# Attention and a Fourier feed-forward block: 120 matmuls of a constant tile added to the plan of the first phase

## The chip, the cores and the metric

The kernel runs on one core of a Trainium2 chip. The metric is the device time of one execution in microseconds (us); the median of several executions counts. An execution with the hardware profiler on left the profile that is read here.

## The reference, cut to what matters

```python
# q, k, v: (8, 8, 576, 64); w_ch1: (512, 2048); w_ch2: (2048, 512); everything in float32
kv  = einsum('bhsd,bhse->bhde', k, v)
out = einsum('bhsd,bhde->bhse', q, kv)
x   = out / sqrt(mean(out * out, -1) + 1e-6) * g_norm      # then (8, 576, 512)
X   = fft(fft(x, axis=1), axis=2)                          # over rows, then over columns
u   = x + real(X)
un  = (u - mean(u)) / sqrt(var(u) + 1e-6)
return u + maximum(un @ w_ch1, 0) @ w_ch2
```

## The kernel before

There are eight batches of 576 rows. For each batch the first phase does these steps. `plan_kv` loads k and v in four pairs of heads (L460) and multiplies them into `ps_k` (L481); the buffers of these loads are a ring of six, `RINGS["kv"]`. `plan_q_load` and `plan_q` load q in two sides (L504, L510), turn it on TensorE into `ps_q` (L529), and copy it on ACT (L533). `plan_out` multiplies it with kv into `ps_o` (L554); ACT copies and squares that (L569, L574), DVE sums it (L578), POOL multiplies it by the norm weights (L589). `plan_y` works out the root, `plan_fold` scales the rows and folds them by their symmetry: DVE (L651, L662), POOL (L669), then ACT makes the rounded half `xh` (L675) and POOL the rest `xl` (L678). `plan_seq` is the DFT over rows (`ps_f`, L693), `plan_chn` that over columns (L727), and `plan_turn` turns the result (`ps_t`, L813) into the blocks `unTh` and `unTl` for the feed-forward part.

The weights arrive as raw 64-bit numbers and are decoded on ACT (L285) and DVE (L292 to L302, L857), centred by a mean on TensorE (`ps_w`, L315), and split in two parts. Each feed-forward product is three fp32r matmuls (`passes`): `ffn1` (L354) makes `ps_h`, `ffn2` (L372) makes `acc`. `plan_early` does the first three of sixteen weight blocks for a block of 512 rows inside the first phase, as work that fills holes: its rank is `FILL + 10 * j` with `FILL = 1000`, while the steps of a batch have ranks from 0 to 77. After the first phase a plain loop does the rest.

The order of the first phase is made by `Plan`. Each step has an engine, a cost in ns, a rank, the steps it comes after, and the ring buffers it takes. `Plan.run` goes forward in time: whenever an engine is free it gives it the ready step of the lowest rank whose buffers are free, and emits that step's instructions. A step on another engine becomes ready `HOP` = 150 ns after the last step that it waits for. So the order on each engine follows from these costs. Tile's scheduler then keeps this order but for single instructions that are ready earlier than those ahead of them. Each engine runs its queue in order, and SP issues nearly all loads and stores.

All PSUM tiles are one ring of eight banks (`p8`, by `bank_buf`).

Of the kernel before, what the change touches and what calls it, by code (L numbers as in the profile page):

```python
# [10 lines left out]
F32R = mybir.dt.float32r  # L11
# [16 lines left out]
NA = 3  # L28
NB1 = 4
NSEG = 4  # L30


SLACK = 2000
# [23 lines left out]
class Plan:  # L57
# [16 lines left out]
    def op(self, eng, cost, rank, emit, after=(), bufs=(), lag=0, port=False, wait=0):  # L74
        o = Op()
        o.port = port or eng == "POOL"
        o.wait = wait
        o.eng, o.cost, o.rank, o.emit, o.lag = eng, cost, rank, emit, lag
        o.after = [a for a in after if a is not None]
        o.bufs = list(dict.fromkeys(bufs))  # L80
        for b in o.bufs:
            b.left += 1
        o.n = len(self.ops)
        o.done, o.dma = None, False
        self.ops.append(o)
        return o

    def dma(self, kb, rank, emit, after=(), bufs=(), eng="SP"):
        o = self.op(eng, 600, rank, emit, after, bufs, lag=kb * 4)
        o.dma = True  # L90
        return o
# [94 lines left out]
def kernel(  # L186
# [14 lines left out]
    nc = tc.nc  # L201
# [3 lines left out]
    P = 128  # L205
# [8 lines left out]
    KC = DM // P  # L214
# [24 lines left out]
    op, dma = plan.op, plan.dma  # L239

    def bank(name):
        return psum.tile([P, BT], F32, name=name, tag="p8", bufs=8)

    def bank_buf(name):
        return Buf("p8", lambda: bank(name))

    ident = perm.tile([P, P], F32, name="ident")
# [137 lines left out]
    cst = ph1.enter_context(tc.tile_pool(name="cst", bufs=1))  # L385
    one = ph1.enter_context(tc.tile_pool(name="one", bufs=1))
    two = ph1.enter_context(tc.tile_pool(name="two", bufs=2))

    gb = cst.tile([P, D], F32, name="gb")
    cs = cst.tile([TR + 1, 2, 2, 3, NS], F32R, name="cs")  # L390
    cd = cst.tile([P, 2, 2, 2, ND], F32R, name="cd")
    x0 = cst.tile([TR + 1, 3, B], F32, name="x0")
# [8 lines left out]
    def rank(b, stage):  # L401
        return 10 * b + stage

    KV, QT, OUT, SCL, FOLD, SEQ, CHN, NRM = range(8)
    URGENT = -100
    FILL = 1000
# [5 lines left out]
    i_gb = dma(32, rank(0, QT), lambda: nc.sync.dma_start(gb, g_norm.partition_broadcast(P)))  # L412
    i_row = dma(18, rank(2, 0), lambda: nc.sync.dma_start(rowidx, order))

    dft = {}

    def plan_dft(part, dst, src, n, r, key):
# [680 lines left out]
    F1 = NA + NB1  # L1098
    early = [NBLK - 2, NBLK - 1] + list(range(NBLK - 3, NBLK - 1 - NSEG, -1))
    blocks = early[::-1][: len(early) - 2] + early[:2] + list(range(1, NBLK - NSEG)) + [0]  # L1100
    segs = [(j, NA, F1) for j in early]
# [197 lines left out]
```

## Time and profile before

| | us |
|---|---|
| median of 3 runs | 1025.22 |
| lowest, highest | 1022.89, 1028.03 |
| the profiled execution | 1026.22 |
| its span, from the first to the last instruction | 1024.4 |
| PE busy in it | 993.9 |
| DVE, ACT, POOL busy | 472.0, 322.4, 320.6 |

PE is TensorE's matmul, PEld its weight load, DVE is VectorE, ACT ScalarE, POOL GpSimd, SP SyncE; SPq and ACTq are the DMA issues of these engines. L481 is line 481 of the kernel. The views used are the page's totals; a table of stages, with the busy time of each engine in each stretch of the span; the timeline of an engine, which merges instructions that follow each other; and the chain of work that ended last, followed back from the end. Matmuls are pipelined, so the durations of single ones overlap; the distance from one start to the next is their pace. A matmul of 64 columns in float32 appears as two instructions.

### The profile page before, as it was taken

How to read it: one execution, taken by the hardware profiler on the slowest of the kernel's cores; microseconds unless marked ns; L12 is line 12 of the kernel's file. 1: busy time of each engine (PE TensorE's matmuls, PEld its weight loads, DVE VectorE, ACT ScalarE, POOL GpSimd, SP SyncE). 2: the span in 40 equal slices, each digit the busy share in tenths (PEclk: the TensorE clock that was granted, in tenths of full speed). 3: DMA queues.
4: the chain of work that ended last, by engine and by line, in shares of the span. 5: the costliest groups of instructions: out<-in, count | busy, mean ns of one | idle time of the engine just before them, and what ended most of it. 6: DMA issues, size and time to landing. Idle time of an engine off the chain costs nothing.

```text
span 1024.4 us, 15026 instructions
## 1 busy us (share of the span) xinstructions
PE 993.9 (97%) x5866; PEld 839.4 (82%) x5866; DVE 472.0 (46%) x838; ACT 322.4 (31%) x655; POOL 320.6 (31%) x332
## 2 busy tenths in 40 slices
PE   4698999999999999999999999999999999999998
PEld 4697898889888888888888888888888888888886
DVE  4758775654588689998131314131221311311211
ACT  2456565555545434334221212021121021210110
POOL 0555876864865131225722303020020010110000
PEclk9998999999999999999999999999999999999999
DMA  9979979663246766645552515140320400400101
GB/s 245 253 164 280 190 214 263 168 182 139 88 162 212 275 206 253 228 136 175 155 177 74 182 51 170 71 139 1 125 81 0 165 21 1 164 1 1 42 1 41
DMA packets 109194, 140.70 MB, mean 137 GB/s; under 512 B 51790, under 2 KB 76418, under 8 KB 104516
## 3 DMA queue, kind: packets, MB, share of 16 engines
q1 hardware_dynamic: 105588, 132.28, 42.4%
q0 software_dynamic: 1920, 6.29, 2.0%
q10 hardware_dynamic: 1616, 1.18, 0.4%
q8 instruction: 46, 0.75, 0.3%
q14 instruction: 24, 0.20, 0.1%
HBM read 88.33 MB, written 51.40 MB: 136 GB/s over the span
## 4 chain that ended last, share of the span: by engine, by line
PE 93%; DMA 2%; DVE 2%; SPq 1%; issue 1%; ACT 0%; POOL 0%; DVEq 0%; ACTq 0%; POOLq 0%
PE ps_h L354 38%; PE acc L372 38%; PE ps_o L554 4%; PE ps_f L727 3%; PE ps_f L693 3%; PE ps_k L481 3%; PE ps_q L529 2%; PE ps_t L813 2%; DMA vm<-in_v_dram 2%; DVE x L651 1%; DMA qt<-in_q_dram 1%; SPq L510 1%; PE ps_w L315 0%; SPq L460 0%; DVE unTl L825 0%
## 5 line engine op out<-in xcount | busy, mean ns | idle before, releaser
L354 PE MATMUL ps_h<-unTh,w 128*128 128x512 f32 x1152 | 357.1, 391 | 0.0
L372 PE MATMUL acc<-w,hh 128*128 128x512 f32 x1152 | 345.0, 391 | 0.2 <-DVE unTl L825 0.2
L367 DVE SCALAR_TENSOR_TENSOR hl<-ps_h,hh 128x512 fp32r<-128x512 f32 x144 | 99.2, 689 | 379.8 <-ACT hh L364 377.5
L354 PEld LDWEIGHTS ps_h<-unTh,w 128*128 128x128 f32 x1152 | 215.4, 188 | 44.0
L372 PEld LDWEIGHTS acc<-w,hh 128*128 128x128 f32 x1152 | 214.9, 188 | 44.3 <-issue 0.3
L364 ACT ACTIVATE hh<-ps_h 128x512 fp32r<-128x512 f32 x144 | 85.9, 597 | 472.1 <-PE ps_h L354 442.9
L354 PE MATMUL ps_h<-unTl,w 128*128 128x512 f32 x576 | 224.5, 390 | 0.0
L372 PE MATMUL acc<-w,hl 128*128 128x512 f32 x576 | 213.1, 390 | 0.0
L354 PEld LDWEIGHTS ps_h<-unTl,w 128*128 128x128 f32 x576 | 108.3, 188 | 22.7
L372 PEld LDWEIGHTS acc<-w,hl 128*128 128x128 f32 x576 | 107.9, 188 | 22.5
L1133 POOL DMA_INDIRECT uu<-u_scr,rowidx x24 | 23.4, 974 | 286.2 <-DVE uu L1186 175.6
L589 POOL TENSOR_TENSOR x<-x,gb 96x512 f32<-96x512 f32 (+1 forms) x48 | 61.9, 1308 | 55.2 <-ACT x L569 40.6
L1152 POOL TENSOR_TENSOR uu<-uu,up 128x512 f32<-128x512 f32 x36 | 45.7, 1293 | 44.5 <-ACT up L1149 44.5
L554 PEld LDWEIGHTS ps_o<-kvt,fq 64*96 64x96 f32 (+1 forms) x768 | 42.7, 185 | 5.6 <-issue 3.2
L554 PE MATMUL ps_o<-kvt,fq 64*96 64x64 f32 (+1 forms) x768 | 47.0, 274 | 0.3 <-ACT fq L533 0.3
L481 PE MATMUL ps_k<-vm,km 128*64 128x64 f32 x512 | 28.7, 261 | 17.6 <-DMA vm<-in_v_dram 16.7
L1096 POOL TENSOR_TENSOR w<-wap,w 128x512 fp32r<-128x512 f32 x18 | 23.3, 1295 | 70.1 <-ACT w L1095 70.1
L1186 DVE SCALAR_TENSOR_TENSOR uu<-acc,rs_yb,uu 128x512 f32<-128x512 f32 x36 | 25.2, 745 | 42.5 <-PE acc L372 42.5
L578 DVE TENSOR_REDUCE ss<-ps_o 96x8 f32<-96x512 f32 (+1 forms) x48 | 32.2, 682 | 26.2 <-ACT ps_o L574 26.0
L669 POOL TENSOR_TENSOR xe<-ab 96x256 f32<-96x256 f32 (+1 forms) x48 | 37.5, 803 | 19.8 <-DVE ab L662 19.7
L693 PE MATMUL ps_f<-cs,xh 96*128 96x290 f32 (+1 forms) x192 | 41.8, 312 | 0.4 <-DVE x L651 0.4
L481 PEld LDWEIGHTS ps_k<-vm,km 128*64 128x64 f32 x512 | 22.9, 166 | 22.4 <-DMA km<-in_k_dram 16.2
(103 smaller groups left out, 1009.1 us busy)
## 6 DMA issues: line engine op xcount, KB each, us to landing
raw<-in_moe_w_ch_dram SPq DMA_DIRECT2D x32, 512.0 KB, 7.6
qt<-in_q_dram SPq DMA_DIRECT2D x16, 576.0 KB, 9.2
unT_scr<-unTh SPq DMA_DIRECT2D x9, 1024.0 KB
unT_scr<-unTl SPq DMA_DIRECT2D x9, 1024.0 KB, 6.3
part_scr<-part SPq DMA_DIRECT2D x36, 256.0 KB, 4.1
unTh<-unT_scr SPq DMA_DIRECT2D x9, 1024.0 KB, 4.9
unTl<-unT_scr SPq DMA_DIRECT2D x9, 1024.0 KB, 7.0
up<-part_scr SPq DMA_DIRECT2D x36, 256.0 KB, 3.0
```

The lines of the kernel that those rows point to most:

```text
L354: nc.tensor.matmul(ps, w[c][:, kc * P : (kc + 1) * P], unT[a][:, kc, :], start=(idx == 0), stop=(idx == 3 * KC - 1),)
L364: nc.scalar.activation(hh, ps, AF.Relu)
L367: nc.vector.scalar_tensor_tensor(hl, ps, 0.0, hh.bitcast(F32), ALU.max, ALU.subtract)
L372: nc.tensor.matmul(acc, hpair[a][:, i * P : (i + 1) * P], w[c], start=(first and n == 0), stop=(last and n == 2),)
L481: nc.tensor.matmul(ps.t[s * D : (s + 1) * D, pr * D : (pr + 1) * D], km[:, s, j, :] if j < 4 else kr[:, h, :], vm[:, s, j, :] if j < 4 els ...
L554: nc.tensor.matmul(pss[s].t[:n, at : at + D], fqs[side].t[half, m, :n], kvt.t[half, m], start=True, stop=True,)
L578: nc.vector.tensor_reduce(ss.t[0][:n, :, t, s::2], pss[s].t[:n].rearrange("p (u m e) -> p u m e", u=2, e=D), AX.X, ALU.add,)
L589: nc.gpsimd.tensor_tensor(v_, v_, gb[:n].unsqueeze(1).to_broadcast([n, H, D]), ALU.mult)
L669: nc.gpsimd.tensor_tensor(o[:, s], a[:, 0], a[:, 1], ALU.subtract if s else ALU.add)
L693: nc.tensor.matmul(ps.t[:, :NS], xs[t].t[a][:n, part, ch * P : (ch + 1) * P], cs[:n, part, c, t, :], start=(idx == 0), stop=(idx == 8),)
L727: nc.tensor.matmul(ps.t[:n, :ND], pt.t[a][:, part, ch, offs[t] : offs[t] + n], cd[:, part, c, ch, :], start=(idx == 0), stop=(idx == 5),)
L1152: nc.gpsimd.tensor_tensor(us[j][i], us[j][i], part, ALU.add)
```

## The change

A step `TICK` of 12000 ns on an engine of its own and a copy of the identity into the tile `still` on DVE are what 60 new PE steps wait for. Each does two matmuls of `still` with itself, repeated four times along the columns. All write one bank: `ps` is made once, taken by the first of them and given back after the last. Their cost is 454 ns, their rank `FILL * 20` = 20000, above that of all others. Nothing reads that bank. The new steps come into being ahead of all steps of the batches.

```diff
+SPARE = 60
+SPARE_FROM = 12000
...
+    still = cst.tile([P, P], F32R, name="still")
...
+    def plan_spare():
+        i_still = op("DVE", 200, URGENT, lambda: nc.vector.tensor_copy(still, ident))
+        bell = op("TICK", SPARE_FROM, 0, lambda: None)
+        ps = bank_buf("ps_s")
+        wide = still.unsqueeze(1).to_broadcast([P, KC, P])
+
+        def go():
+            for _ in range(2):
+                nc.tensor.matmul(ps.t, still, wide, start=True, stop=True)
+
+        for _ in range(SPARE):
+            op("PE", 454, FILL * 20, go, [i_still, bell], [ps])
+
+    plan_spare()
```

## Rows read from the trace of the kernel before

**Rows 1.** The page: busy time of PE, and the granted clock by slice.

```profile
PE 993.9 (97%) x5866; PEld 839.4 (82%) x5866; DVE 472.0 (46%) x838; ACT 322.4 (31%) x655; POOL 320.6 (31%) x332
...
PEclk9998999999999999999999999999999999999999
```

**Rows 2.** Table of stages: stretch, length, busy us of engines, PEclk, DMA share, GB/s.

```profile
45.39:66.30 20.91, 20.91 (x173) 18.96 (x174) 10.39 (x17) 11.68 (x26) 13.27 (x14) 1.00 1.00 218
...
88.96:91.99 3.03, 0.00 (x1) 0.03 (x1) 3.00 (x6) 3.03 (x7) 1.32 (x2) 0.71 0.96 302
91.99:97.00 5.01, 5.01 (x36) 4.49 (x37) 5.01 (x10) 2.55 (x7) 1.80 (x2) 0.50 0.98 341
97.00:1024.40 927.40, 921.50 (x5065) 774.57 (x5064) 409.52 (x732) 273.71 (x550) 278.06 (x278) 1.00 0.40 128
```

**Rows 3.** PE's timeline: start, us, line, tiles, count, idle before and its releaser.

```profile
12.77 1.12 PE L481 MATMUL ps_k<-vm,km 128*64 128x64 f32 x16 [0.89 <-DMA km<-in_k_dram]
...
18.86 2.16 PE L529 MATMUL ps_q<-ident,qt 97*128 97x97 f32 x12 [4.55 <-DMA qt<-in_q_dram]
...
45.39 1.12 PE L481 MATMUL ps_k<-vm,km 128*64 128x64 f32 x16 [8.27 <-DMA vm<-in_v_dram]
...
91.99 1.12 PE L481 MATMUL ps_k<-vm,km 128*64 128x64 f32 x16 [3.03 <-DMA vm<-in_v_dram]
```

**Rows 4.** Chain that ended last, up to 110 us: start, us, what, instructions.

```profile
27.32 5.43 PE ps_o L554 x64
...
46.93 2.76 PE ps_q L529 x16
...
54.30 1.46 PE ps_k L481 x20
...
69.78 1.75 PE ps_k L481 x40
...
80.29 0.66 PE ps_q L529 x8
...
84.39 1.50 PE ps_o L554 x32
85.89 0.82 PE ps_t L813 x8
```

**Rows 5.** PE's timeline in the DFT over rows: its start, the rise, its end.

```profile
60.64 0.85 PE L693 MATMUL ps_f<-cs,xh 97*128 97x290 f32 x2
...
66.35 0.30 PE L693 MATMUL ps_f<-cs,xl 96*128 96x290 f32 x1
...
67.96 0.29 PE L693 MATMUL ps_f<-cs,xl 96*128 96x290 f32 x1
```

**Rows 6.** PE's timeline in feed-forward matmuls: the first ones, and ones from the middle.

```profile
95.34 1.20 PE L354 MATMUL ps_h<-unTh,w 128*128 128x512 f32 x2
96.34 0.63 PE L354 MATMUL ps_h<-unTl,w 128*128 128x512 f32 x1
...
800.92 0.62 PE L354 MATMUL ps_h<-unTh,w 128*128 128x512 f32 x2
...
811.12 0.62 PE L354 MATMUL ps_h<-unTh,w 128*128 128x512 f32 x2
```

**Rows 7.** Timelines of SP, DVE, ACT and POOL; the load is from the chain.

```profile
35.48 4.74 SPq L460 DMA_DIRECT2D km<-in_k_dram  x1
...
40.27 4.99 DMA vm<-in_v_dram
...
12.44 0.70 DVE L292 TENSOR_SCALAR ps_a<-ps_a 128x512 f32<-128x512 f32 x1 [11.38 <-ACT ps_a L285]
...
50.35 1.14 ACT L675 ACTIVATE xh<-xe 97x512 fp32r<-97x512 f32 x2
...
57.84 1.26 POOL L678 TENSOR_TENSOR xl<-xe,xh 96x512 fp32r<-96x512 f32 x1
```

## What I expect of the change

> **What bounds the kernel now.** I read the page's totals first, then a table of stages, then PE's timeline and the chain that ended last. The totals say that PE is busy nearly all the time [rows 1], so the end is set by PE's work plus what PE loses. The stage table says where it loses [rows 2]: from 97 us on PE is busy for 921.50 of 927.40 us, and most of the rest is the tail behind the last matmul. So all that matters lies ahead of 97 us, and a shift of the first feed-forward matmuls is a shift of the end.
>
> Ahead of 97 us there are two kinds of loss. The first is idle time: the four large waits are 0.89, 4.55, 8.27 and 3.03 us, all for loads [rows 3]. The second isn't seen in the busy time: pace. The chain gives it, start to end of a run of matmuls [rows 4]. A pair of kv (20 instructions) takes 1.46 us at 54 us and 1.75/2 = 0.875 at 70. A transpose takes 2.76/16 = 0.172 us at 47, and 0.66/8 to 0.82/8, some 0.09, after 80. An out instruction takes 5.43/64 = 0.085 us at 27 and 1.50/32 = 0.047 at 84. The sequence DFT shows the moment: 23 matmuls from 60.64 to 66.35 at 0.248 us each, then 12 in 1.61 us, 0.134 each [rows 5]. That is the 1.2 GHz level against the 2.4 GHz level. The page's clock row prints nearly full speed there [rows 1], and so does the stage table for 45.39 to 66.30 [rows 2]; I go by the pace, which doubles at 66.35 with no change of shape. So TensorE runs at half clock from its first matmul to 66.35 us, and again from some 91 to 97, after the idle 3.03 us, where the table does print 0.50 [rows 2].
>
> On that clock row the Trainium skill (TensorE: Matmul & The Clock Gate, Part 1, Seeing it yourself) warns that recorded clock events have been unreliable on trn2 and are to be checked against other figures; the pace above agrees. The same part (What's actually happening) holds the loss from warming up to be under 1% of a typical span. By that rule the half clock would be worth at most some 10 us here instead of the 17.0 below, and the sum would come out some 7 us slower (an estimate from that page).
>
> **The change part by part.** It adds 60 planner steps of two 128x128 by 128x512 matmuls, 120 in all; one copy of 128x128 on DVE, which sits idle until 12.44 us, so I cost it at nothing (without that cover, a quarter of the 0.70 us that a 128x512 step takes [rows 7]); 512 bytes a partition; and one PSUM bank that all 60 share, held from the first to the last. By the planner's own count at least three of the eight banks are free up to plan time 49, so the bank costs nothing (without that, an out step, which takes two, would be put off by the time of a copy and a square on ACT). Nothing reads the result, so no engine waits for it. What the spares cost is their place in PE's queue: q, out and kv of batches 0 and 1 stand behind them.
>
> *What one costs.* The feed-forward matmuls have this shape: 45 of them from 800.92 to 811.12, 0.2267 us each at full clock; at half clock two took 1.00 us, 0.50 each [rows 6]. 120 x 0.2267 = 27.2 us. The first run at half clock. How long until it rises is bounded by two rows: the DFT ran 5.7 us before it rose [rows 5], the feed-forward matmuls from 95.34 some 1.5 us [rows 6]. That is 3 to 11 matmuls with an excess of 0.27 us, 0.8 to 3.1 us. I take 2.0, since the spares have the shape of the second and come, as the first, after a long stretch at half clock. So 29.2 us.
>
> *Where they go.* Their rank is below all else and a step of 12000 holds them back, so the planner puts them into every hole of its PE from plan time 12.15 us on, 0.454 us each, rounded up. Its holes, worked out from its own costs, in order: ahead of the last kv pair of batch 0 (5 steps), between that and the first q (10), among q, out and the weight mean of batch 0 (3, 2, 6), ahead of the four kv pairs of batch 1 (8, 4, 8, 4), around q of batch 1 (6, 4). That is 60: they are used up at plan time 47, far ahead of the first feed-forward step at plan time 87. So none guards the wait of 3.03 us, and that loss stays. Since they wait for nothing once they have the bank, Tile's scheduler can only pull them ahead of these places; as the sum is made at q of batch 1, with nearly all of them past, that changes it little.
>
> *What they meet.* The first 15 steps take 30 x 0.2267 + 2.0 = 8.8 us and find 0.89 + 4.55 = 5.4 us of idle [rows 3]: q starts 3.4 us late, but at full clock. From there to the end of batch 1's third kv pair, at 37.06, PE had no idle worth the name, and gets 31 steps, 14.1 us. In return its work there runs at full clock: three kv pairs save 1.8 us, 24 transposes 2.0, 96 out instructions 3.6, a weight mean 0.4: 7.8 [rows 4]. Does the clock hold through such small matmuls? From 76.2 to 88.9 us PE does nothing but q, out, kv and transposes and one weight mean, at the fast pace to the end [rows 4], so yes. PE then reaches the fourth pair, with its 4 steps (1.8 us), at 37.06 + 3.4 + 14.1 - 7.8 + 1.8 = 48.6 instead of 45.39: the 8.27 us are filled and PE is 3.2 late. Ten more steps add 4.5. The work up to 66.35 saves 1.8 (kv), 2.0 (q), 64 x 0.038 = 2.4 (out), 0.4 and 23 x 0.114 = 2.6 (DFT): 9.2. By PE alone it is 3.2 + 4.5 - 9.2 = 1.5 us ahead at that point.
>
> *What is late next.* The DFT needs xl, which POOL finishes for the third row tile at 57.84 + 1.26 = 59.1, only 1.5 us before PE takes it up; POOL waits for xh on ACT, and on ACT xh (50.35) stands behind the copies of batch 1's transposes [rows 7]. Those start 3.2 + 2.7 = 5.9 us later (six of the ten steps stand ahead of them), so xl ends near 65.0. From there PE has 28 DFT matmuls left at 0.134, to 68.8, against 68.1 before (67.96 and one more). What PE had won turns into a wait for POOL of 2.2 us. **Sum: +29.2 (spares) - 17.0 (clock) - 13.7 (idle filled) + 2.2 (new wait) = +0.7 us.**
>
> *The loads.* The kv ring has six buffers, so the load of batch 1's fourth pair waits for its first pair on PE, which ended at 34.1 and now ends at 39.5 (3.4 late, 19 steps or 8.6 us, less 6.0 of q, out and mean and 0.6 of its own). Before, its k load was issued at 35.48 and blocked SP for 4.74 us; its v load went out at 40.27 and landed at 45.26 [rows 7]. So 5.4 us of delay cost from 0 (the block covers it) to 5.4 at the landing. I take 0.3 at the end, since the block lasted to 40.2 and PE itself comes to the pair at 48.6. Behind it on SP stand the loads of batch 2, which PE wants from 54 us on.
>
> The profiled execution took 1026.22 us (span 1024.4), 1.0 over the median of the runs. +0.7 + 0.3 on the median of 1025.22 gives **1026.2 us**.
>
> **The rivals.** *The forecast*: the spares pay for themselves and no more, 1021 to 1030. For it: after 97 us PE has no slack that could swallow or multiply a shift.
>
> *Slower: the ring hands the delay to the loads.* If the v load lands the whole 5.4 us later, at 50.7, PE waits 2.1 us at the fourth pair, and xl and the DFT move by as much. If that wait also drops the clock, as 3.03 us of idle did [rows 3], the ten steps behind it run partly at half clock again (0.8 to 3.1 us) with the kv pair and q among them (up to 2.6). Sum 1.0 + 2.1 + 5 = some +8: 1033. It decides from the point where the wait ahead of that pair reaches 2 to 3 us. Against: the queue was blocked up to 40.2 anyway. Were none of the old idle filled, the bound is 13.7 above the forecast: 1040.
>
> *Faster: the fill is free.* If Tile pulls the last ten steps ahead of the fourth pair, and xh goes ahead of the copies on ACT, PE keeps its 1.5 us; if the shifted loads also remove the wait at 88.96 and the half clock behind it (3.03 + 2.3), it is -7: 1018 to 1024. The floor by this count is all four waits gone: 29.2 - 17.0 - 16.7 - 2.3 = -6.8. Against: spares that are used up by plan time 47 don't touch the last wait.
>
> *It doesn't do what it says:* the clock doesn't rise on a constant tile. Then 120 x 0.50 = 60 us against 13.7 of idle: about 1072. Against: nothing in the trace ties the clock to values.
>
> **How the numbers follow.** Forecast 0.54; slower, by the ring or by an order that came out worse, 0.31; faster 0.13; no rise 0.02. Faster by over 0.5% (below 1020.1; half a per cent is about what a measurement of this kernel can tell from no change) is the far half of the faster case and some luck in the planner's order: 0.11. Slower by over 0.5% (above 1030.3) is most of its case, the last one and the forecast's edge: 0.32. Within: 0.57. For 8 in 10 I leave out about 0.08 below 1019 and 0.12 above 1036.
>
> **What would show it.** Right: kv pairs of batch 1 at 0.87 us instead of 1.46; some 15 spare steps around the last pair of batch 0; the fourth pair of batch 1 at 46 to 49 us with hardly a wait; the DFT at 0.134 from its start, with a wait for POOL in it; the first feed-forward matmul within 2 us of 95.3, and a wait of some 3 us ahead of it still there. Wrong: spares beyond 60 us, or an out step that waits for a bank; a first feed-forward matmul far from 95; new idle after 97.

## The result, and the profile after

The changed kernel takes 1029.05 us (median of 11 runs, 1027.62 to 1030.47) against 1025.22 before (11 runs as well): a ratio of 1.0036, 95% interval 1.0021 to 1.0051. That is a small loss, just over a third of a per cent by the ratio, and 2.9 us above the forecast of 1026.2. Four executions of the last group of experiments were far slower than the rest (1119.94 and 1685.75 us, and two of the kernel before) and are in no median, range or ratio here. The profiled execution took 1028.0 us with a span of 1026.2, which is 1.8 above that of before.

The page of the kernel after, totals and clock row:

```profile
PE 1009.6 (98%) x5986; PEld 848.5 (83%) x5986; DVE 469.6 (46%) x839; ACT 321.1 (31%) x655; POOL 323.8 (32%) x332
...
PEclk9999899999999999999999999999999999999999
```

PE has the 120 matmuls more and is busy 15.7 us more than in [rows 1]; the span grew by 1.8. The other 13.9 us went into idle time. The table of stages of the kernel after (columns as in [rows 2]) shows where:

```profile
12.00:20.00 8.00, 8.00 (x45) 6.14 (x45) 5.23 (x7) 1.36 (x3) 0.00 (x0) 1.00 1.20 216
...
40.00:90.00 50.00, 50.00 (x616) 43.09 (x616) 35.92 (x65) 28.17 (x65) 33.20 (x39) 1.00 0.87 213
90.00:100.00 10.00, 8.88 (x88) 7.17 (x87) 10.00 (x18) 8.02 (x21) 4.62 (x7) 1.00 0.98 346
100.00:114.00 14.00, 11.19 (x95) 9.02 (x94) 13.97 (x21) 5.53 (x12) 13.30 (x15) 0.76 1.18 219
```

From 12 to 100 us PE hardly waits any more; the waits of 0.89, 4.55, 8.27 and 3.03 us [rows 3] are gone. Instead 2.81 us are missing between 100 and 114, and the clock column falls to 0.76 there. PE's timeline of the kernel after, in four places (line, tiles, count, idle before and its releaser):

```profile
11.55 6.61 PE L428 MATMUL ps_s<-still 128*128 128x512 f32 x21
18.09 0.69 PE L500 MATMUL ps_k<-vm,km 128*64 128x64 f32 x16
18.97 2.34 PE L428 MATMUL ps_s<-still 128*128 128x512 f32 x9
...
44.17 3.92 PE L428 MATMUL ps_s<-still 128*128 128x512 f32 x16
48.02 0.69 PE L500 MATMUL ps_k<-vm,km 128*64 128x64 f32 x16
...
92.45 0.73 PE L358 MATMUL ps_h<-unTh,w 128*128 128x512 f32 x2 [0.36 <-ACT fq L552]
...
105.56 0.33 PE L500 MATMUL ps_k<-vr,kr 64*64 64x64 f32 x4 [2.81 <-DMA vr<-in_v_dram]
...
109.12 1.22 PE L358 MATMUL ps_h<-unTh,w 128*128 128x512 f32 x2
...
115.51 0.43 PE L712 MATMUL ps_f<-cs,xh 97*128 97x290 f32 x2
```

The first 21 spares take 6.54 us to the next start, 18.09: they are slow at first, fast at the end. Behind them sixteen kv matmuls take 0.69 us where [rows 3] has 1.12. The first feed-forward matmuls start at 92.45, 2.9 us ahead of before [rows 6], and at full clock. Then PE runs into a wait for `vr` of the next batch, and behind it the same matmuls take 1.22 for two, the half clock. In the kernel before, PE took the same `vr` at 106.15 without a wait:

```profile
106.15 0.33 PE L481 MATMUL ps_k<-vr,kr 64*64 64x64 f32 x4
...
113.20 0.43 PE L693 MATMUL ps_f<-cs,xh 97*128 97x290 f32 x2
```

The DFT over rows of batch 1, the first step behind all of this, starts at 115.51; in before it started at 113.20. From that point on the two kernels have the same 4895 matmul instructions left, by the table of stages of each.

So the account is made up to that DFT. The starts of the runs of spares show what they take: 31.0 us. Idle time up to 114 us fell from 24.6 to 11.1, a gain of 13.5. The start moved by 2.3. What is left, 31.0 - 13.5 - 2.3 = 15.2 us, is put down to the pace of the kernel's own work.

### The profile page after: what moved, and what is told of

Read it like the earlier page. It is cut to its first block, busy times and chain, and to the rows that moved or that the text cites. A ratio compares the mean times of both kernels' runs of the same rounds, so it can differ in the third digit from the quotient of the medians.

```text
span 1026.2 us, 15268 instructions
## 1 busy us (share of the span) xinstructions
PE 1009.6 (98%) x5986; PEld 848.5 (83%) x5986; DVE 469.6 (46%) x839; ACT 321.1 (31%) x655; POOL 323.8 (32%) x332
## 4 chain that ended last, share of the span: by engine, by line
PE 93%; DMA 2%; DVE 2%; SPq 1%; ACT 1%; issue 1%; POOL 0%; DVEq 0%; ACTq 0%; POOLq 0%
PE ps_h L358 38%; PE acc L376 38%; PE ps_f L712 3%; PE ps_f L746 3%; PE ps_o L573 3%; PE ps_k L500 3%; PE ps_t L832 2%; PE ps_s L428 2%; PE ps_q L548 1%; DMA vr<-in_v_dram 1%; DMA draw<-in_dft_s_dram 1%; DMA km<-in_k_dram 1%; SPq L529 0%; DVE x L670 0%; PE ps_w L319 0%
## 5 line engine op out<-in xcount | busy, mean ns | idle before, releaser
L573 PEld LDWEIGHTS ps_o<-kvt,fq 64*96 64x96 f32 (+1 forms) x768 | 38.0, 163 | 5.6 <-issue 3.1
L573 PE MATMUL ps_o<-kvt,fq 64*96 64x64 f32 (+1 forms) x768 | 42.0, 251 | 0.2 <-DVE w L885 0.2
L712 PE MATMUL ps_f<-cs,xh 96*128 96x290 f32 (+1 forms) x192 | 39.1, 300 | 0.0
L1159 DVE BATCH_NORM_STATS2 bst<-uu 128x6 f32<-128x512 f32 x36 | 24.4, 686 | 28.1 <-DMA uu<-u_scr,rowidx 18.8
L746 PE MATMUL ps_f<-cd,pt 128*96 128x258 f32 (+1 forms) x288 | 36.9, 284 | 0.2 <-DVE x L670 0.2
```

The lines of the kernel that those rows point to most:

```text
L573: nc.tensor.matmul(pss[s].t[:n, at : at + D], fqs[side].t[half, m, :n], kvt.t[half, m], start=True, stop=True,)
L712: nc.tensor.matmul(ps.t[:, :NS], xs[t].t[a][:n, part, ch * P : (ch + 1) * P], cs[:n, part, c, t, :], start=(idx == 0), stop=(idx == 8),)
L746: nc.tensor.matmul(ps.t[:n, :ND], pt.t[a][:, part, ch, offs[t] : offs[t] + n], cd[:, part, c, ch, :], start=(idx == 0), stop=(idx == 5),)
```

## The experiments

A number beside a ratio is the median of the runs of that kernel; each group of kernels was run on one chip with the kernel before beside it, and the ratio on record, with its 95% interval in brackets, is to those runs (it is close to the quotient of the two medians, but not the same). The median of the kernel before was 1026.16 beside the runs with fifteen steps, with narrow spares, with the first try at the new wait and with the stores in the plan; 1025.91 beside the two with the stores tied and the two with 92 matmuls that follow them; and 1026.73 beside the other four. Times of different groups are compared by these ratios only.

### Only the first fifteen steps

```diff
-SPARE = 60
+SPARE = 15
```

> SPARE = 15 in place of 60: only the spare steps around the last kv pair of batch 0 stay, the 45 steps (20.4 us at full clock) among the work of batches 0 and 1 go. Theory 'displaced work' (the changed kernel loses because 45 of the 60 steps stand where TensorE had no idle time): 20.4 us less on TensorE, of which 8 reopen as the wait for batch 1's fourth kv pair, so some 10 us faster than the changed kernel, 1017 to 1021. Theory 'clock falls again' : TensorE reaches that pair at some 33 us, waits 12 us for a load that lands at 45.3, drops to half clock, and from there on repeats the kernel before: 1024 to 1028, the DFT over rows of batch 0 at 0.24 us a matmul in its first part. Theory 'loads bind' (the loads of batch 4 land at 105.4 us whatever TensorE did before): the same time, 1024 to 1030, but with a wait at 100 to 106 us if the clock did hold.

1027.33 us, ratio 1.0010 (0.9994 to 1.0027): no change. PE's timeline:

```profile
18.82 0.69 PE L500 MATMUL ps_k<-vm,km 128*64 128x64 f32 x16
...
26.83 1.55 PE L573 MATMUL ps_o<-kvt,fq 64*96 64x64 f32 x16 [3.21 <-ACT fq L552]
...
37.85 1.12 PE L500 MATMUL ps_k<-vm,km 128*64 128x64 f32 x16
```

The fifteen steps bring the clock up (0.69 at 18.82), and the first long wait behind them takes it away: PE waits 3.21 us for ACT up to 26.83, and from there on it is slow again, 1.12 for a kv row of sixteen, up to 70 us. The time is that of the theory 'clock falls again', but the clock fell at an earlier wait than that theory had named, one that the kernel before does not have. So the first quarter of the spares brought no gain by itself; in the kernel after the next spares stand where this wait is.

### Narrow instead of wide spares

```diff
-        wide = still.unsqueeze(1).to_broadcast([P, KC, P])
+        wide = still[:, :64]
...
-            for _ in range(2):
-                nc.tensor.matmul(ps.t, still, wide, start=True, stop=True)
+            for _ in range(8):
+                nc.tensor.matmul(ps.t[:, :64], still, wide, start=True, stop=True)
```

> The same 60 planner steps at the same planned cost, but each of eight matmuls of 64 columns instead of two of 512. If it is the clock that the spares buy, and narrow matmuls don't raise it (the narrow ones of the kernel before didn't in 18.86 to 37.06 us): 480 matmuls at 0.066 to 0.09 us, 32 to 43 us, for 13.7 us of idle and nothing back, with the DFT over rows still at 0.24 us a matmul: 1040 to 1055. If the spares' effect is that of their place in the queue alone: as the changed kernel, 1027 to 1033.

1118.02 us, ratio 1.0882 (1.0861 to 1.0904). PE's timeline:

```profile
22.17 17.27 PE L428 MATMUL ps_s<-still 128*128 128x64 f32 x80
...
139.92 1.89 PE L428 MATMUL ps_s<-still 128*128 128x64 f32 x8
141.74 1.12 PE L500 MATMUL ps_k<-vm,km 128*64 128x64 f32 x16
```

A matmul of 64 columns took 0.217 us, where 512 columns take 0.2267 at full clock [rows 6]; 480 of them are 104 us. Each has a weight load of its own, 0.33 us long in this trace, so 0.217 is the pace of matmul and load together. The kv row still takes 1.12 us at 141.74: PE's timeline has no gap from 12 us on, and yet the clock had not come up. My expectation had 0.066 to 0.09 us for one and was far off. Of the two forms tried, the wide one alone brought the clock up.

### Holding the clock in the new wait

First 12 constant matmuls in the kv step of batch 4:

```diff
+                    if held and j == 4:
+                        wide = still.unsqueeze(1).to_broadcast([P, KC, P])
+                        for _ in range(12):
+                            nc.tensor.matmul(held[0].t, still, wide, start=True, stop=True)
```

> The changed kernel with 12 more matmuls of the constant tile ahead of the last part of batch 4's first kv pair, where TensorE waits 2.81 us for a load that lands at 105.4 and then runs at half clock until 113.6. Theory 'loads bind, and the wait costs twice': the 12 matmuls (2.7 us) lie in the wait, the clock holds, the DFT over rows of batch 1 starts at 112.5 to 113 instead of 115.5, and the time is 2 to 3.5 us below the changed kernel, 1025.5 to 1027. Rival 'the late loss is made up later by feed-forward work': the time stays at 1028 to 1030.

1027.24 us, ratio 1.0014 (1.0000 to 1.0027), between the two theories. Tile's scheduler moved the 12 ahead of the second feed-forward group, to 98.15, so that they filled part of the gap but did not stand in it; the wait shrank to 1.30 us, and the half clock behind it stayed in the profiled execution. In the twelve executions the time goes with the mean granted clock: 1025.8 to 1027.7 where it was 0.998 or more, 1029.1 to 1030.9 where it was 0.996 or less.

The second time an order edge on TensorE tied them between the pair's instructions on `vm` and those on `vr`:

```diff
+                    if j == 4 and held:
+                        with tc.issue_after(last.ins):
+                            for _ in range(12):
+                                last = nc.tensor.matmul(held[0].t, still, wide, ...)
```

> After, with 12 more matmuls of the constant tile inside the first kv pair of batch 4, between its 16 instructions on vm and its 4 on vr, tied there by an order edge on TensorE: they go into the 2.81 us in which after waits for vr at 102.75 to 105.56. (In e2_hold the same 12 came at 98.15, ahead of four feed-forward groups, and did not reach that wait.) They cost 12 x 0.227 = 2.7 us, all inside the wait. Theory 'the clock falls in that wait': the half clock at 106.7 to 113.9 goes; by after's rows it cost some 0.4 on the kv pair, 0.5 on 12 out instructions and 2.2 on eleven feed-forward matmuls, 3.1 us together: 1026, the ratio to before 1.0005 to 1.001. Rival 'the fall is due to something else, or comes elsewhere in other executions': 1029 as after, ratio 1.0036, with half clock behind the pair or at another wait.

1027.54 us, ratio 1.0016 (0.9994 to 1.0038). PE's timeline:

```profile
93.77 0.52 PE L561 MATMUL ps_q<-ident,qt 96*128 96x96 f32 x4 [2.35 <-DMA qt<-in_q_dram]
...
101.51 3.03 PE L506 MATMUL ps_z<-still 128*128 128x512 f32 x12
...
107.68 0.33 PE L512 MATMUL ps_k<-vr,kr 64*64 64x64 f32 x4
...
110.87 0.73 PE L359 MATMUL ps_h<-unTh,w 128*128 128x512 f32 x2
```

Here `vr` is met without a wait and the feed-forward matmuls behind are fast, though PE also comes 2.1 us later than in the kernel after, and Tile has again put four feed-forward groups behind the 12. For in this execution another load, `qt` at 93.77, came 2.35 us late, and the clock fell behind that wait. The executions whose mean clock was 0.999 or more took 1025.6 to 1026.9, as the first theory said; those below 0.996 took 1030.2 to 1036.2. That fits a worth of some 3 us for the half clock at 106.7 to 113.9. By the rows it is 3.0: the same kv pair, twelve out instructions and twelve feed-forward matmuls take 7.45 us there and would take some 4.4 at the pace of the kernel before. That the slower executions lose their clock elsewhere is shown for the profiled one alone.

### The store ahead of the late load

On SP the loads of batch 4's first pair stand behind the stores of the first turned block. The first attempt made these stores wait for the loads in the plan:

```diff
-                turned, [unT],
+                turned + (kv_lds[4] if j == 0 else []), [unT],
```

> The changed kernel, but the two 1 MB stores of block 0's unT, which SP issued at 92.15 and 92.66 us just ahead of the loads of batch 4, wait in the plan until those loads are done. Theory 'loads bind': k and v of batch 4 land some 5 us earlier, the wait of 2.81 us ahead of 105.56 and the half clock behind it go, 1022 to 1026. Rival 'ring or SP issue, not the transfers in front, sets the landing': it stays at 105 and the time at 1028 to 1031.

1027.11 us, ratio 1.0007 (0.9996 to 1.0019). SP's order did not change up to 107 us, and the stores still went out ahead of the loads, so it did not test what it was for. It shows the scatter of the same order: in its profiled execution `vr` was 1.93 us late, the clock held, and the span was 1022.4.

The second attempt tied the stores behind the loads on SP, in the kernel after and, as a control, in the kernel before:

```diff
+            with tc.issue_after(max(kv_lds[4], key=lambda o: o.n).ins.ins):
+                keep(c)
...
+                turned + ([] if j else kv_lds[4]), [unT],
```

> The changed kernel with the two 1 MB stores of block 0's unT really behind the first loads of batch 4 on SP (in the earlier try of this SP still issued them at 92.15 us, ahead of those loads, so it tested nothing). Theory 'loads bind': v of batch 4's first pair lands 4 to 6 us before 105, TensorE no longer waits 2.81 us there, the clock holds in every execution, 1022 to 1025. Rival 'the loads in front (q and kv of batch 3) set the landing': it stays at 104 to 105, 1027 to 1030.

> The kernel before with the same move of the two stores. In it TensorE reaches the same pair at 106.15 without a wait, so under 'loads bind' the move buys nothing there: the wait of 3.03 us at 88.96 and the half clock after it stay, within 2 us of the kernel before. Rival 'those stores cost the kernel in any case' (transfers behind them, q of batch 4 among them, come earlier): 3 us or more faster than the kernel before.

The kernel after with it: 1027.98 us, ratio 1.0016 (1.0000 to 1.0033). By its time the expectation of 1022 to 1025 failed; by its trace 'loads bind' holds. The chain that ended last, from issue to landing of `vr`, first after, then with the stores moved, and behind that PE's timeline with the stores moved:

```profile
95.85 9.58 DMA vr<-in_v_dram
```

```profile
94.48 5.23 DMA vr<-in_v_dram
```

```profile
99.75 0.33 PE L501 MATMUL ps_k<-vr,kr 64*64 64x64 f32 x4 [0.74 <-DMA vr<-in_v_dram]
...
110.52 0.43 PE L714 MATMUL ps_f<-cs,xh 97*128 97x290 f32 x2
...
387.17 0.46 PE L319 MATMUL ps_w<-wap,mean_t 128*128 128x128 f32 x2 [2.12 <-DVE wap L311]
```

The load lands 5.7 us earlier, PE takes the pair up with 0.74 us of wait, and the DFT of batch 1 starts 5.0 us earlier than after. It goes out 1.4 us earlier, and its transfer is 4.3 us shorter, 5.23 instead of 9.58. So it was this load that PE waited for, and it was late because of the stores ahead of it. But of the 5.0 us only 2.0 reach the end of the profiled execution (span 1024.2): at 387.17 PE now waits 2.12 us for DVE, which decodes the weights. DVE had itself waited 2.73 us, up to 384.14, for the load of `uu`, so this second border is a load again.

The kernel before with the same move: 1025.11 us, ratio 0.9992 (0.9975 to 1.0009), no change. There `vr` was waited for by 0.21 us only, and a wait of 3.17 us for `vm` at 91.42 with half clock behind it stayed.

### The last wait of the kernel before, by itself

Thirteen constant matmuls ahead of batch 3's fourth pair, tied behind the last transpose of q that was made before them, and no other spare. The difference is shown against the kernel after; the copy into `still` stays as well:

```diff
-SPARE = 60
+SPARE = 0
...
+            more = {(3, NPAIR - 1): 13}.get((b, pr), 0)
...
+                    with tc.issue_after(turned_last[0].ins) if b == 3 else nullcontext():
+                        for _ in range(more):
+                            nc.tensor.matmul(held[0].t, still, wide, start=True, stop=True)
```

> The kernel before with only 13 matmuls of the constant tile, ahead of batch 3's fourth kv pair, where before waited 3.03 us at 88.96 to 91.99; no others. They cost 13 x 0.227 = 2.9 us, all inside the wait. It tells what the last wait's half clock is worth by itself, without the spares of the change. Theory 'that wait drops the clock': the half clock at 92 to 97 goes, 2.3 us by before's rows: 1022.9, ratio 0.9978. Rival 'other waits behind it drop the clock in its place': 1025, ratio 1.000.

1027.07 us, ratio 1.0007 (0.9989 to 1.0024): no gain. PE's timeline:

```profile
87.06 3.19 PE L504 MATMUL ps_s<-still 128*128 128x512 f32 x13
90.29 0.69 PE L510 MATMUL ps_k<-vm,km 128*64 128x64 f32 x16
...
92.50 0.71 PE L359 MATMUL ps_h<-unTh,w 128*128 128x512 f32 x2
...
104.03 0.33 PE L510 MATMUL ps_k<-vr,kr 64*64 64x64 f32 x4 [2.20 <-DMA vr<-in_v_dram]
...
111.81 0.43 PE L726 MATMUL ps_f<-cs,xh 97*128 97x290 f32 x2
...
402.35 0.49 PE L320 MATMUL ps_w<-wap,mean_t 128*128 128x128 f32 x2 [0.49 <-DVE wap L312]
```

The wait of 3.03 us and the half clock behind it [rows 2, 3] are gone, and the first feed-forward matmuls start at 92.50, as in the kernel after. That is 2.8 us ahead of before, but 1.4 of it this execution had already at 69 us, ahead of the thirteen matmuls: its early loads came sooner, and the DFT of batch 0 started at 58.71 instead of 60.64. Then PE waits 2.20 us for the same `vr` as the kernel after, which before met without a wait. The DFT of batch 1 is 1.4 us earlier, the lead of 69 us and no more: what the thirteen matmuls won went to this load. SP had its last long wait for PE ahead of that load up to 85.2, before the thirteen matmuls, so the load came no earlier for them. The 1.4 us go too: PE is still 1.4 ahead at 395.74 (before: 397.12) and 0.1 at 402.59 (before: 402.71), and between them it waits for DVE, 0.23 us at 400.66 and 0.49 at 402.35. The span is 1024.4, that of before. The expectation's rival, no gain, came true, but not by a clock that fell elsewhere: the mean clock of this execution is 0.998, against 0.996 before, and it held behind the 2.20 us.

### Fewer spares, most of them in the wait

The first 52 matmuls as after, then 40 ahead of batch 1's fourth pair, the place of the 8.27 us [rows 3], none between the pairs ahead of it and none behind it. Tile moved nine of the 40 ahead, among the out instructions of batch 0; 31 stand in the wait:

```diff
-SPARE = 60
+SPARE = 26
...
+            held = [spare_ps] if b == 1 and pr == NPAIR - 1 else []
...
+                    for _ in range(40):
+                        nc.tensor.matmul(held[0].t, still, wide, start=True, stop=True)
```

> 92 instead of 120 matmuls of the constant tile: the ones around the last kv pair of batch 0 and among q and out of batch 0 stay, none between the first three kv pairs of batch 1, 31 in one block in the wait ahead of the fourth, none after it. Theory 'displaced work': 28 fewer, 6.7 us less on TensorE, 1020 to 1023. Theory 'loads bind': TensorE is earlier up to 90 us and then waits longer, in front of batch 3's last pair or batch 4's first, with the clock falling there: 1025 to 1030, no better than the changed kernel by more than 3 us.

1023.06 us, ratio 0.9986 (0.9961 to 1.0011). PE's timeline:

```profile
38.99 7.32 PE L501 MATMUL ps_s<-still 128*128 128x512 f32 x31
46.24 0.69 PE L507 MATMUL ps_k<-vm,km 128*64 128x64 f32 x16
...
57.38 0.54 PE L719 MATMUL ps_f<-cs,xh 97*128 97x290 f32 x2
...
86.50 1.12 PE L507 MATMUL ps_k<-vm,km 128*64 128x64 f32 x16 [3.73 <-DMA vm<-in_v_dram]
...
114.14 0.43 PE L719 MATMUL ps_f<-cs,xh 97*128 97x290 f32 x2
```

With 28 matmuls less the fourth pair starts at 46.24 instead of 48.02 and the DFT at 57.38 instead of 62.88, 5.5 us earlier, still at full clock. So most of those 28, some 6.7 us at 0.24, had stood in front of work that was ready. The DFT of batch 1 is only 1.4 us earlier than after, but PE has done more by then: by the table of stages 4854 matmul instructions are left there, against 4895 in before and after. This lead isn't taken back by the loads, since it moves them. SP's issues in this run, and in the kernel after:

```profile
64.89 0.37 SPq L480 DMA_DIRECT2D km<-in_k_dram  x1
...
89.85 1.40 SPq L489 DMA_DIRECT2D vr<-in_v_dram  x1
```

```profile
70.59 0.37 SPq L479 DMA_DIRECT2D km<-in_k_dram  x1
...
95.85 1.45 SPq L488 DMA_DIRECT2D vr<-in_v_dram  x1
```

Up to the first of these SP stands blocked for a buffer of the kv ring that PE has to give back. PE gives it back 5.7 us earlier here, and `vr` goes out 6.0 us earlier. The span of 1019.3 is 6.9 below that of after, although PE waits 3.73 us at 86.50 and loses the clock for 5 us. The executions fall into two groups, 1019.1 to 1021.8 with a mean clock of 0.995 to 0.997 and 1024.3 to 1030.7 with 0.988 to 0.992, six each. The median is at the upper edge of what 'displaced work' had forecast. It is the best of all versions by its ratio, and better than after; that it beats the kernel before isn't shown, since the interval holds 1.

With the stores moved as well:

> The 92 matmuls of the run just described together with the stores behind the first loads of batch 4. 'Loads bind': 1020 to 1024, better than either alone and than the kernel before. 'Displaced work' alone: the same as with the 92 matmuls and the stores where they were.

1025.14 us, ratio 0.9992 (0.9970 to 1.0014), with the lowest time of all, 1018.61, and two groups again: five executions of 1018.6 to 1023.0 and seven of 1025.0 to 1029.5. The median missed the 1020 to 1024 of 'loads bind', and a gain over the 92 matmuls alone isn't shown.

### Holding the clock there too

The last two add 14 constant matmuls ahead of batch 3's fourth pair, tied behind the last transpose or out step made before them, to the two kernels above.

> e6_clean with 14 more matmuls of the constant tile ahead of batch 3's fourth kv pair, where e6_clean waited 3.73 us for vm at 82.8 to 86.5 and then ran at half clock to 92. They cost 14 x 0.227 = 3.2 us, all inside that wait. Theory 'the spread of e6_clean (1019.1 to 1030.7) is whether a wait of this kind drops the clock and for how long': the half clock goes, which cost some 0.7 on the kv pair, 0.75 on eight transposes and 1.3 on the first feed-forward matmuls, 2.7 us: a profiled span of 1016 to 1017, and most executions at 1016 to 1021, ratio 0.993 to 0.996. Rival 'the slow executions of e6_clean lose their clock in other waits (those for ACT and loads in the first 60 us)': the spread stays, 1016 to 1030, median 1021 to 1024, ratio 0.996 to 0.999.

> e7_both (e6_clean with block 0's stores of unT behind batch 4's first loads) with the same 14 matmuls ahead of batch 3's fourth kv pair. By the clock theory 2.5 us below e7_both's better executions (1018.6 to 1023.0): 1016 to 1020, ratio 0.992 to 0.996; if the stores behind the loads hold up the feed-forward rows of the next block, or the slow executions lose the clock elsewhere, 1021 to 1028 in part of them, ratio 0.997 to 1.001.

1026.29 us, ratio 1.0006 (0.9983 to 1.0029), and 1029.68, ratio 1.0024 (1.0004 to 1.0045). Both expectations failed. The first one's timeline of PE:

```profile
55.23 0.33 PE L505 MATMUL ps_k<-vr,kr 64*64 64x64 f32 x4 [2.00 <-DMA vr<-in_v_dram]
...
58.28 3.20 PE L591 MATMUL ps_o<-kvt,fq 64*96 64x64 f32 x32
...
92.02 3.75 PE L591 MATMUL ps_o<-kvt,fq 64*97 64x64 f32 x32 [1.41 <-DVE wa L324]
95.70 5.67 PE L518 MATMUL ps_s<-still 128*128 128x512 f32 x14
```

Both profiled executions lost the clock at two other places: a load that came late (2.00 us at 55.23 here, 1.64 at 54.82 in the second), and a wait of 1.41 us for DVE (92.02 and 91.57). The 14 matmuls that were to hold the clock ran mostly at half clock themselves, 5.67 us instead of 3.2. So holding one wait doesn't hold the kernel. But the two runs do not change that wait alone: the shared bank is now taken up to batch 3 instead of batch 1, which leaves the plan one bank less for some 50 us, and neither wait stands in the profiled execution with the 92 matmuls alone. Whether the bank or the scatter of the loads made them is not shown.

## Why the prediction came out right, and where it didn't

The time was right within 2.9 us, inside the range and in the likeliest case, a change of less than half a per cent. The sum had +29.2 - 17.0 - 13.7 + 2.2 = +0.7; the traces have +31.0 - 15.2 - 13.5 = +2.3 up to the DFT of batch 1, and +1.8 at the end. The medians differ by 3.8. Term by term the sum missed by +1.8 (spares), +1.8 (pace), -2.2 (the wait for POOL) and +0.2 (idle time), and the last of these is small only because a wait that I kept went away and one that I didn't have came. The mechanism, spares that pay for themselves in filled waits and a faster clock and no more, was right up to the DFT of batch 0. Behind it the path to the end was not the one that I had drawn, and that misses of some 2 us each leave so little is luck. Of my signs of being right, the first feed-forward matmul within 2 us of 95.3 and the wait of some 3 us ahead of it failed, and a sign of being wrong, new idle after 97, came.

**What a spare costs.** Nearly right. The first 21 took 6.54 us; at 0.2267 they would take 4.8, so the half clock added 1.8, where I took 2.0. The other 99 took 0.247 instead of 0.2267 each. Each of their eleven runs, of 5 or of 20, is 0.11 to 0.24 us longer than its matmuls at 0.2267, so the loss is at the edges between spares and small matmuls, 2.0 us together, which the sum did not have.

**Where they go.** Right in the main: 30 matmuls, fifteen steps, around the last pair of batch 0, the rest in the holes up to 56.0 us, none near the first feed-forward rows. Behind that the counts differ a little: 36 up to batch 1's first pair (38 forecast), then 8, 6 and 16 ahead of the next three (8, 16, 8), and 24 behind the fourth (20). So four more than forecast stand behind it, though I had said that Tile could only pull them ahead.

**What they bring up to the DFT.** Right. The kv pairs run at 0.88 us, the fourth starts at 48.02 without a wait (forecast 48.6), and the clock holds through q, out and kv. So the 0.3 us that I had added for the loads did not come at that pair. The rival in which the ring hands its delay to that pair fell with this.

**The wait for POOL.** Wrong, by 2.2 us. I had read POOL as waiting for `xh` on ACT, behind the copies of batch 1's transposes, and had left that order as it was in [rows 7]. For the third row tile this reading was wrong already in the kernel before. Its `xh` was done at 56.2, and its `xl` at 57.84 stood behind two multiplications by the norm weights on POOL itself (L589), a term that the sum did not have. The planner makes these orders anew: with PE's out steps later, the multiplications come behind the last `xl`. POOL's timeline before, and after:

```profile
55.38 2.49 POOL L589 TENSOR_TENSOR x<-x,gb 96x512 f32<-96x512 f32 x2 [0.16 <-ACT x L569]
```

```profile
52.63 1.29 POOL L697 TENSOR_TENSOR xl<-xe,xh 97x512 fp32r<-97x512 f32 x1
...
55.27 2.51 POOL L697 TENSOR_TENSOR xl<-xe,xh 96x512 fp32r<-96x512 f32 x2
...
58.77 2.51 POOL L608 TENSOR_TENSOR x<-x,gb 96x512 f32<-96x512 f32 x2 [0.94 <-ACT x L588]
```

The last `xl` ends at 57.8, 1.3 us earlier than before, and the DFT starts at 62.88 and runs at 0.134 from its third matmul to its end. The slack that I gave, 1.5 us, is to the start of the DFT; PE takes the third tile's `xl` only at 62.73 in the kernel before, 3.6 us behind its end.

**The last wait.** Wrong, in its place and not in its size. I had said that the 3.03 us at 88.96 and the half clock behind it stay, since no spare stands there. SP's queue was made anew too, and PE's order: it takes batch 3's first pair at 76.55 instead of 80.88. The load of `vm` for batch 3's fourth pair, on SP before and after:

```profile
86.96 0.46 SPq L460 DMA_DIRECT2D vm<-in_v_dram  x1
```

```profile
80.06 1.37 SPq L479 DMA_DIRECT2D vm<-in_v_dram  x1
```

It goes out 6.9 us earlier, and the pair at 88.61 doesn't wait. The gain that the faster rival had named for this, some 5 us, came, and was lost again at once: `vr` of batch 4 goes out at 95.85 after, and at 95.72 before:

```profile
95.72 1.47 SPq L469 DMA_DIRECT2D vr<-in_v_dram  x1
```

PE, now 3.4 us earlier there, waits 2.81 us for it and loses the clock for 7 us behind. The step that failed is that I followed the loads only as far as batch 2, and took a shift of the first feed-forward matmuls for a shift of the end. The first paragraph of the prediction, by which all that matters lies ahead of 97 us, put the border too early: it lies at least behind this load, at 106 us. Moving the stores showed it, and the thirteen matmuls in the kernel before showed that the same load takes the gain there. On the way to that load SP waits long for PE twice: at batch 2's kv pairs, up to 70.59 after and 70.43 before, and ahead of `vr`, up to 88.36 after and 86.91 before. PE was no earlier at either, since the spares had eaten by then what they had brought. With 28 fewer of them the two waits ended at 64.89 and 80.89, and the loads followed. The weights that DVE decodes near 385 to 405 us are a second border of this kind: 2.12 us with the stores moved, 1.3 in the run with thirteen matmuls.

**The clock.** Of the forecast 17.0 us some 16 came up to 66 us. The 15.2 hold that, and also the 2.3 of half clock that went at 92 to 97 and the 3.0 that came new at 106.7 to 113.9. These 15.2 us are 1.5% of the span. The Trainium skill (TensorE: Matmul & The Clock Gate, Part 1, What's actually happening) holds the loss from warming up to be under 1% of a typical span. Here the measurement decides against it: in the kernel before PE ran at half clock for 66 us, and not only for its waits, since it was still slow at 37.06 after 18 us with hardly a gap.

**What stays open.** Which of the short waits drops the clock in an execution. Whether holding the clock in the late waits is worth anything with the shared bank left as it was. And how much of the 3.8 us between the medians is the account above: the profiled execution of before lies 1.0 above its median and that of after 1.0 below its own.

## What to carry to other kernels

Filler matmuls buy clock with TensorE's own time. Here they paid only in gaps; those that stood ahead of ready work cost most of their length (5.5 of 6.7 us) and, through the ring of load buffers, moved the loads behind them. Before counting a gain on PE, follow the queue of loads past the place of the gain: a gain that comes ahead of the point where that queue waits for TensorE moves the loads with it, and one behind that point can be taken back by the next load, and the wait there can cost the clock as well. A planner that orders by ranks and costs makes the queues of other engines anew when one engine's work moves, so an order read from the old trace is not evidence for the new one.

## What the runs showed of the hardware that I had not expected

In some of these kernels the time of an execution goes with its mean granted clock: in the twelve executions of the kernel with 92 spares a line through time and clock falls by 1.1 us for each thousandth of mean clock (correlation 0.95), and in the eleven with the tied matmuls in the wait for `vr` by 1.0 (0.95). A thousandth of the time is 1.0 us. So in these two kernels most of the scatter between executions goes with the granted clock. It isn't so in all: in the kernel before the correlation is 0.4 to 0.7 by group, and in the eleven runs of the kernel after it is 0.2.

In these runs the length of a wait does not tell whether the clock fell behind it. It held behind 1.93 us (store in the plan, 104.52) and 2.20 us (the kernel before with thirteen matmuls, 104.03); it fell behind 1.30 us (the first try at the new wait, 105.67), 1.41 and 2.00 us (the first of the last two runs) and 2.81 us (after).

The recorded clock can't be compared between kernels. The run with fifteen steps has a mean of 0.975 and before 0.996, at the same time within 0.2%. The half clock of before up to 66 us, which its pace shows [rows 5], isn't in the record, while the fall at 26.83 us in the other run is. The run with narrow spares prints 0.995, though it was at half clock to 156 us. So the record seems to print full speed until its first event.
